# Turning attention outputs by DMA and a layer norm by TensorE in a fused transformer block, with a new order

## The chip, the cores and the metric

One core of one Trainium2 chip. The time is device microseconds (us) of one launch; that of the kernel before is the median of three runs. A profile is one execution taken by the hardware profiler.

The engines: TensorE (PE; its weight loads are listed apart as PEld), VectorE (DVE), ScalarE (ACT), GpSimd (POOL), and SyncE (SP), which here only issues DMAs. Each engine runs its own instructions in the order of the program and waits on semaphores.

## The reference

A transformer block with pre-norm, forward and backward, in bf16, for 2048 tokens of width 512 (32 heads of 16, feed-forward width 1792):

```python
def _A_ref(x, wqkv, wo):            # dilated sliding window: 8 keys, 2 apart
    q, k, v = qkv[0], qkv[1], qkv[2]                       # x @ wqkv
    idx = pos[:, None] - off[None, :]                      # off = arange(8) * 2
    logits = jnp.einsum("bhsd,bhswd->bhsw", q, kg) * scale
    attn = _softmax(jnp.where(mask[None, None, :, :], logits, -1e9), axis=-1)
    o = jnp.einsum("bhsw,bhswd->bhsd", attn, vg)
    return o.transpose(0, 2, 1, 3).reshape(B, S, D) @ wo

def _B_ref(x, w1, b1, w2, b2):
    h = _gelu(jnp.einsum("bsd,df->bsf", x, w1) + b1)
    return jnp.einsum("bsf,fd->bsd", h, w2) + b2

h = x + _A_ref(_layernorm(x), A_wqkv, A_wo)
h2 = h + _B_ref(_layernorm(h), B_w1, B_b1, B_w2, B_b2)
# outputs: h2 and the gradients of x, wqkv, wo, w1, b1, w2, b2 for a given grad_out
```

## The kernel before

The tokens are cut into four chunks of 512 (`c` from 0 to 3, four tiles of 128 rows each). Per chunk the forward pass runs `p1_ln` (first layer norm), `p1_qkv`, `p1_attn`, `p1_o` (attention output), `p1_h` (output projection with `wo`, residual `h`, second layer norm `ln2`), `p2_h` (first feed-forward matmul with `w1`, GELU), `p2_out` (second one, `w2`). The chunks are worked in the order 0, 2, 1, 3. The backward pass is `p2_dg`, `p2_bwd` (matmuls with `w2T` and `w1T`), `p3_go`, `p3_dots`, `p3_bands`, `p3_gl1` (gradient of x, tile `gx`), and `wg_ffn` makes the weight gradients.

Attention is made of bands: VectorE multiplies (`prod`, tile `prbo` in the forward pass), PE sums with a 0/1 matrix (`bsum`, L527), ScalarE copies the sum out (`sink`, L532, tile `ost`). A matmul needs its left operand with the width along the partitions, so `ost` has to be turned into `oT`, and `ln2` into `ln2T`. There are two ways:

- by PE: 16 transposes of 128x128 for each chunk into PSUM, and copies by ScalarE. `turn` (L543) does it for `ost` in two halves of 1024 columns, `to_fm_tiles` (L416) for a layer norm in four tiles of 512.
- by DMA: one transposing transfer of 512 KB on SyncE's queue, `turned` for `ost` and `to_fm_dma` for a layer norm (both through `xload`, L291).

Constants at the end of the file choose the way for each chunk: `FMO` lists the chunks whose `ost` is turned by DMA, `FM2` those whose `ln2` is.

Every step is recorded as an operation first. `emit` then writes the operations out in the order of the table `ORDER`, made ahead of time outside the kernel, with the addresses of `HOMES`. That sets the order on every engine and queue. `emit` also decides the form of most matmuls:

```python
            if o.eng == "PE":
                if o.cls == 4:
                    run.append(i)
                else:
                    if prev == 1 and o.cls == 1:
                        quad.update(run)
                    run, prev = [], o.cls
```

Class 1 operations (band sums, attention sums, the q and k projections) are always issued as four matmuls of 32 columns side by side. A run of ordinary matmuls (class 4) that stands between two class 1 operations is issued in the same form, as four strips (L268); all others are issued full, with 128 columns (L270). A transpose on PE is class 0 and ends a run.

DMA transfers of SyncE's and ScalarE's queues finish on a shared, rotating set of eight semaphores, so an issue may also wait until an earlier transfer has landed, on whichever queue that was.

Of the kernel before, what the change touches and what calls it, by code (L numbers as in the profile page):

```python
# [13 lines left out]
ACT = mybir.ActivationFunctionType  # L14
# [145 lines left out]
def kernel(  # L160
# [30 lines left out]
    NC = S // CH  # L191
# [767 lines left out]
    def p3_gl1(c):  # L959
# [6 lines left out]
        for j in range(TPC):  # L966
# [9 lines left out]
            if j == 0:  # L976
                gx = sb("gx", [P, TPC, D])
            ln_bwd(t, NT + t, j % 2, pair, ps, rstdp, RP, ln1, lambda j=j: ln1()[:, j, :], [(gh_[c], j - 1), (gh_[c], j)], lambda j=j: gh_[c]()[:, j - 1:j + 1, :],
                   gx, lambda j=j: gx()[:, j - 1:j + 1, :], (j - 1, j), "1")
        for j, ap in enumerate(perm_rows(gxf[c * CH:(c + 1) * CH, :])):  # L980
            store(None, lambda ap=ap: ap, gx, lambda j=j: gx()[32 * j:32 * j + 32], 128, tag="gxst")
# [196 lines left out]
FM2 = (1, 2, 3)  # L1178
# [4 lines left out]
FMO = ()  # L1183
# [146 lines left out]
```

## Time and profile before

| what | value |
|---|---|
| median of three runs | 557.82 us (556.07 to 574.06) |
| profiled execution | 557.15 us |
| its span, first to last instruction | 555.4 us |
| mean granted TensorE clock | 0.999 |
| busy PE / DVE / ACT / POOL | 539.7 / 494.2 / 324.2 / 32.4 us |
| PE matmuls | 5568 |
| DMA moved | 126.40 MB, mean 228 GB/s |

The profiled execution is 1.75 us longer than its span: that lies around the first and the last instruction. A busy PE need not be at its peak, since matmuls are pipelined and their ends are modelled. A name such as `ps<-wo,oT` reads: the tile written, then the tiles read.

### The profile page before, as it was taken

To read this page: it belongs to the slowest core of one execution; us is meant where nothing else is said; L and a number is where in the kernel's file an instruction comes from. 1 tells how busy PE (TensorE), PEld (TensorE's weight loads), DVE (VectorE), ACT (ScalarE), POOL (GpSimd) and SP (SyncE) were. 2 spreads that over 40 slices of the span, in tenths; PEclk is the share of its full clock that TensorE was granted. 3 is DMA by queue.
4 is the path that set the end of the run, shared out by engine and by line. 5 is a ranking of instruction groups with operands and counts; after the bars stand their busy time and mean duration, and the time that the engine had idled before them with its cause. 6 is when DMAs were issued, how large, how long until landed. Compare 5 with 4: busy or idle time off the path is not lost. (4 is left out here: it accounts for less than half of the span.)

```text
span 555.4 us, 13067 instructions
## 1 busy us (share of the span) xinstructions
PE 539.7 (97%) x5568; PEld 268.9 (48%) x5568; DVE 494.2 (89%) x648; ACT 324.2 (58%) x503; POOL 32.4 (6%) x38
## 2 busy tenths in 40 slices
PE   7999999999999999999999999999999998999995
PEld 4655554444444444444444444455455554555442
DVE  7999999999999999889885877789879998999992
ACT  4998699887999794996131324042324556633531
POOL 1610100021001000000000000000010001000000
PEclk9999999999999999999999999999999999999999
DMA  8898998975499617298999989999999999778237
GB/s 265 218 289 251 395 368 236 199 228 185 97 268 281 179 34 167 77 152 221 199 210 184 194 183 187 295 212 271 240 357 374 305 335 372 318 272 162 52 72 199
DMA packets 195306, 126.40 MB, mean 228 GB/s; under 512 B 149744, under 2 KB 190896, under 8 KB 193200
## 3 DMA queue, kind: packets, MB, share of 16 engines
q1 hardware_dynamic: 189760, 82.06, 64.5%
q0 software_dynamic: 3312, 41.42, 19.2%
q10 hardware_dynamic: 2176, 2.10, 1.2%
q8 instruction: 43, 0.70, 0.5%
q14 instruction: 15, 0.12, 0.1%
HBM read 55.74 MB, written 35.21 MB: 164 GB/s over the span
## 5 line engine op out<-in xcount | busy, mean ns | idle before, releaser
L270 PE MATMUL ps<-goT,w2T 128*128 128x512 bf16 x224 | 53.6, 379 | 0.8 <-DVE h2s L828 0.5
L270 PE MATMUL ps<-w1T,xb 128*128 128x512 bf16 x224 | 52.9, 379 | 0.0
L270 PE MATMUL ps<-w,gl 128*128 128x512 bf16 x216 | 50.5, 379 | 0.0
L297 ACT CAST wgs<-ps 128x512 bf16<-128x512 f32 (+1 forms) x30 | 16.2, 558 | 57.4 <-PE ps L268 35.7
L270 PE MATMUL ps<-ln2T,w 128*128 128x512 bf16 x188 | 44.2, 379 | 0.7 <-DVE xb L856 0.3
L774 ACT ACTIVATE xb<-ps,b1c 128x512 bf16<-128x512 f32 x56 | 35.7, 692 | 12.8 <-PE ps L270 12.5
L856 DVE SCALAR_TENSOR_TENSOR xb<-xb,ps 128x512 bf16<-128x512 bf16 x56 | 36.6, 685 | 6.2 <-PE ps L270 5.6
L518 DVE TENSOR_TENSOR prbq<-Rq,cfq 128x4096 bf16<-128x4096 bf16 x16 | 36.0, 2288 | 5.0 <-PE ps L487 1.7
L479 DVE TENSOR_TENSOR prb<-got,vw 128x4096 bf16<-128x4096 bf16 x16 | 36.3, 2282 | 2.7 <-PE ps L487 1.4
L518 DVE TENSOR_TENSOR prbv<-Rv,cfv 128x4096 bf16<-128x4096 bf16 x16 | 36.1, 2283 | 2.7 <-PE ps L268 1.8
L518 DVE TENSOR_TENSOR prbk<-Rk,cfk 128x4096 bf16<-128x4096 bf16 x16 | 36.1, 2283 | 0.7 <-PE ps L527 0.7
L518 DVE TENSOR_TENSOR prbo<-Ro,cfo 128x4096 bf16<-128x4096 bf16 x16 | 35.9, 2288 | 0.4 <-DMA k_d<-tmk 0.2
L479 DVE TENSOR_TENSOR prf<-qt,kt 128x4096 bf16<-128x4096 bf16 x16 | 35.5, 2275 | 0.0
L270 PEld LDWEIGHTS <-w2T 128*128 128x128 bf16 x224 | 21.8, 98 | 27.4 <-issue 2.0
L270 PEld LDWEIGHTS <-xb 128*128 128x128 bf16 x224 | 21.9, 98 | 26.4
L270 PEld LDWEIGHTS <-gl 128*128 128x128 bf16 x216 | 20.8, 98 | 25.6 <-issue 1.6
L796 ACT ACTIVATE xb<-xb 128x2048 bf16<-128x2048 bf16 (+1 forms) x16 | 26.8, 1690 | 7.8 <-DVE xb L795 7.7
L626 PE MATMUL ps<-ln1T,wqk 128*32 128x512 bf16 x512 | 30.2, 383 | 0.0
L270 PEld LDWEIGHTS <-w 128*128 128x128 bf16 x188 | 18.1, 97 | 23.0 <-issue 2.5
L268 PE MATMUL ps<-wqkvT,gqkvT 128*32 128x512 bf16 x448 | 27.4, 379 | 1.7 <-ACT gqkvT L297 1.6
L777 ACT ACTIVATE gl<-xb 128x2048 bf16<-128x2048 bf16 (+1 forms) x16 | 26.8, 1697 | 0.0
L792 ACT ACTIVATE x<-xb 128x2048 bf16<-128x2048 bf16 (+1 forms) x16 | 26.6, 1690 | 0.0
(198 smaller groups left out, 1054.0 us busy)
## 6 DMA issues: line engine op xcount, KB each, us to landing
Ro<-v_d POOLq DMA_DIRECT2D x4, 2304.0 KB, 11.2
Rq<-k_d POOLq DMA_DIRECT2D x4, 2304.0 KB, 11.6
Rv<-go_d POOLq DMA_DIRECT2D x4, 2304.0 KB, 14.2
Rk<-q_d POOLq DMA_DIRECT2D x4, 2304.0 KB, 13.4
g_d<-gl SPq DMA_DIRECT2D x9, 512.0 KB, 3.5
gh_d<-xb SPq DMA_DIRECT2D x9, 512.0 KB, 3.4
w<-in_B_w_dram SPq DMA_DIRECT2D x2, 1792.0 KB, 15.0
out_dram<-wgs SPq DMA_DIRECT2D x13, 256.0 KB, 7.1
```

The costliest lines, as they stand in the source:

```text
L268: T.matmul(out[32 * a:32 * a + 32, :], lhsT=l[:, 32 * a:32 * a + 32], rhs=r, start=start, stop=stop, skip_group_check=True)
L270: T.matmul(out, lhsT=l, rhs=r, start=start, stop=stop, skip_group_check=True)
L297: fn = lambda: A.copy(out=ap(), in_=pap())
L479: op("DVE", tt_us(4096), lambda g=g, pr=pr: V.tensor_tensor(out=pr(), in0=ql()[:, g, :].unsqueeze(1).to_broadcast([P, W, 512]), in1=_sub(k ...
L518: V.tensor_tensor(out=pr().rearrange("p a j (d h) -> p a j d h", h=H), in0=_sub(R()[:, o0, 0:1], [[st, 2], [512, 4], [32, DH], [1, H]]), i ...
L626: T.matmul(ps()[32 * a:32 * a + 32, gg * 512:(gg + 1) * 512], lhsT=_sub(wq_()[:, dc, 0:1], [[DH, H]], sel * D + 4 * g + a), rhs=rhs, start ...
L774: op("ACT", act_us(512, 1), lambda f=f, ps=ps, xb=xb, f0=f0: A.activation(out=xb()[:, f - f0, :], in_=ps(), func=ACT.Identity, bias=b1c[:, ...
L777: op("ACT", act_us(N), lambda xb=xb, gl=gl: A.activation(out=fl(gl), in_=fl(xb), func=ACT.Gelu_apprx_tanh), r=[xb], w=[gl], tag="gelu", mo ...
L792: op("ACT", act_us(N), lambda xb=xb, x2=x2: A.activation(out=fl(x2), in_=fl(xb), func=ACT.Square), r=[xb], w=[x2], tag="x2")
L796: op("ACT", act_us(N), lambda xb=xb: A.activation(out=fl(xb), in_=fl(xb), func=ACT.Tanh, scale=GC), w=[xb], tag="tanh", mode=6)
L856: op("DVE", 0.61, lambda f=f, ps=ps, z=z, f0=f0: V.scalar_tensor_tensor(out=z()[:, f - f0, :], in0=z()[:, f - f0, :], scalar=1.0, in1=ps() ...
```

## The change

The attention outputs of chunks 1 and 3 are turned by DMA, no longer by PE. The second layer norm of chunks 1 and 2 is turned by PE tile by tile, no longer by DMA; chunk 3 stays with DMA and chunk 0 with PE. For chunk 3, two of the four stores of `gx` are issued by ScalarE, no longer by SyncE. `ORDER` and `HOMES` are new as a whole (one line is shown).

```diff
-            store(None, lambda ap=ap: ap, gx, lambda j=j: gx()[32 * j:32 * j + 32], 128, tag="gxst")
+            store(None, lambda ap=ap: ap, gx, lambda j=j: gx()[32 * j:32 * j + 32], 128, q="ACT" if c == NC - 1 and j % 2 else "SP", tag="gxst")
...
-FM2 = (1, 2, 3)
+FM2 = (3,)
...
-FMO = ()
+FMO = (1, 3)
...
 ORDER = (
-    8, 22, 0, 11, 12, 23, 1, 7, 10, 6, 9, 48, 364, 27, 13, 49, 50, 26, 51, 44, 61, 28, 2, 62, 40, 25, 3, 45, 29, 41, 24, 46, 52, 42, 43, 53, 363, 15,
...
```

PE, from the last band sum of chunk 1's attention output (`prbo_432`) to that of chunk 3 (`prbo_581`) and on, before. Repeated rows and the weight loads are left out; `oT1` and `oT3` are the turned outputs of chunks 1 and 3, `gl` the GELU's output, `goT` the turned gradient.

```order
L527 MATMUL ps<-prbo_432_34_1774,S4 32x512
...
L270 MATMUL ps<-wo_91_14_372,oT1_441_32_1803 128x512
...
L543 MATMUL ps<-ident,ost_428_33_1765 128x128
...
L270 MATMUL ps<-ln2T2_478_34_1913,w1_226_24_984 128x512
...
L527 MATMUL ps<-prbo_581_41_2197,S4 32x512
...
L270 MATMUL ps<-ln2T1_533_38_2030,w1_226_24_984 128x512
...
L543 MATMUL ps<-ident,ost_576_42_2169 128x128
...
L270 MATMUL ps<-wo_91_14_372,oT3_628_42_2332 128x512
...
L270 MATMUL ps<-w2_295_21_1264,gl_647_38_2370 128x512
...
L270 MATMUL ps<-w1T_596_41_2268,xb_333_28_1394 128x512
```

The same place in the changed kernel, with `prbo_422` and `prbo_580` as those band sums:

```order
L527 MATMUL ps<-prbo_422_38_1772,S4 32x512
...
L270 MATMUL ps<-wo_60_11_274,oT1_439_33_1841 128x512
...
L416 MATMUL ps<-ident,ln2_2_468_31_1906 128x128
...
L270 MATMUL ps<-ln2T2_479_33_1931,w1_217_22_939 128x512
...
L416 MATMUL ps<-ident,ln2_1_517_35_2013 128x128
...
L527 MATMUL ps<-prbo_580_42_2201,S4 32x512
...
L268 MATMUL ps<-ln2T1_537_38_2056,w1_217_22_939 32x512
...
L268 MATMUL ps<-goT_404_37_1659,w2T_346_34_1440 32x512
...
L268 MATMUL ps<-wo_60_11_274,oT3_600_40_2300 32x512
...
L268 MATMUL ps<-w2_278_24_1161,gl_642_39_2510 32x512
...
L268 MATMUL ps<-w1T_589_40_2249,xb_342_33_1419 32x512
```

The transposes of `ost` (L543) are gone for both chunks, those of `ln2` (L416) are new. Between `prbo_422` and the first `wo` matmul on `oT1` stand 30 full matmuls and 8 transposes of other work, between `prbo_580` and the first on `oT3` 160 strips. Since no transpose ends the run behind `prbo_580`, the whole feed-forward up to the next attention sums is issued in strips: over the program L268 has 5376 matmuls in place of 2448, L270 688 in place of 1420, and PE 15530 rows in place of 11138.

SyncE at the same place, before; `ln2T2` and `ln2T1` are the turned layer norms:

```order
L291 DMA_TRANSPOSE goT_430_33_1768<-gor_256_28_1110 128x16x128
L291 DMA_TRANSPOSE w2T_357_30_1496<-in_B_w2_dram 128x4x448
L287 DMA k_d_58<-tmk_203_29_866 128x2x512
L287 DMA g_d0_73<-gl_419_31_1721 128x2x512
L282 DMA xp3_386_32_1568<-in_A_x_dram 32x4x512
L291 DMA_TRANSPOSE ln2T2_478_34_1913<-ln2_2_465_34_1879 128x16x128
```

And in the changed kernel:

```order
L291 DMA_TRANSPOSE w2T_346_34_1440<-in_B_w2_dram 128x4x448
L287 DMA v_d_57<-tmv_239_27_1031 128x2x512
L282 DMA xp1_93_14_373<-in_A_x_dram 32x4x512
L291 DMA_TRANSPOSE oT1_439_33_1841<-ost_421_38_1770 128x16x128
L287 DMA q_d_59<-tmq_340_33_1409 128x2x512
L287 DMA q_d_59<-tmq_427_35_1793 128x2x512
```

Chunk 1's attention output takes the place that chunk 2's layer norm had, closer behind a transpose of `w2T`; chunk 3's stands between two transposes of `w1T`.

VectorE near the start of the program, before; `xt_0` is chunk 0 of x, `xt_13` chunk 1, `ln_0` the normalised chunk 0:

```order
L360 BN_STATS st<-xt_0_1_95 128x6
L361 BN_AGGR mv<-st 128x2
L369 RECIPROCAL rstd<-ve 128x1
L385 TENSOR_SCALAR ln_0_18_7_133<-xt_0_1_95,mv,rstd 128x512 x2
L369 RECIPROCAL rstd<-ve 128x1
L385 TENSOR_SCALAR ln_0_18_7_133<-xt_0_1_95,mv,rstd 128x512
L360 BN_STATS st<-xt_13_5_126 128x6
```

And in the changed kernel, where chunk 1 is `xt_14`:

```order
L360 BN_STATS st<-xt_0_1_95 128x6
L361 BN_AGGR mv<-st 128x2
L360 BN_STATS st<-xt_14_4_123 128x6
L361 BN_AGGR mv<-st 128x2
L369 RECIPROCAL rstd<-ve 128x1
L385 TENSOR_SCALAR ln_0_23_7_136<-xt_0_1_95,mv,rstd 128x512
```

One statistics pair of chunk 1 now stands ahead of the last normalisations of chunk 0.

204 rows, old and new, of tables (HOMES, ORDER) are left out of this document.

## The prediction

> **What bounds the kernel now.** I read the page's engine shares first, then stretches of the span, then who TensorE waits for, then the chain that ended last.
>
> ```profile
> PE 539.7 (97%) x5568; PEld 268.9 (48%) x5568; DVE 494.2 (89%) x648; ACT 324.2 (58%) x503; POOL 32.4 (6%) x38
> ```
>
> TensorE (PE) is busy for 539.7 of 555.4 us and idle for 15.7. VectorE has 494.2 us of work beside it. So an edit can gain only what is idle or slow inside PE's time. The stretches say where that is (us of the stretch, then busy us and instructions of PE, weight loads, VectorE, ScalarE, GpSimd, then clock, DMA share, GB/s):
>
> ```profile
> 0.00:14.00 14.00, 11.18 (x106) 6.03 (x110) 10.13 (x33) 6.56 (x15) 2.22 (x9) 1.00 0.85 266
> 84.00:98.00 14.00, 13.73 (x133) 6.99 (x134) 13.65 (x10) 13.94 (x19) 0.60 (x1) 1.00 0.83 233
> 112.00:126.00 14.00, 13.13 (x73) 6.28 (x72) 12.68 (x25) 11.23 (x14) 3.52 (x4) 1.00 0.75 234
> 440.00:460.00 20.00, 18.38 (x292) 9.92 (x285) 18.97 (x12) 10.05 (x16) 2.12 (x4) 1.00 1.01 333
> 540.00:556.00 16.00, 9.47 (x44) 4.12 (x42) 5.47 (x13) 2.92 (x5) 0.00 (x0) 0.96 0.73 190
> ```
>
> The start costs 14.00 - 11.18 = 2.8 us and the end 15.4 - 9.47 = 5.9 us (the span covers 15.4 of that stretch). That leaves 15.7 - 2.8 - 5.9 = 7.0 us of idle in the middle, in small pieces in the first 140 us, where VectorE is just as full (13.65 of 14), and one of 1.6 at 440 to 460. The longest waits of PE confirm it:
>
> ```profile
> PE ps L268 <- ACT gqkvT L297: 1.6, 1, 1.6
> PE ps L416 <- DVE ln L385: 1.5, 1, 1.5
> ```
>
> PE's own rate depends on how its instructions follow each other. These pieces are from the chain that ended last (start, us, what, count):
>
> ```profile
> 381.53 0.55 PE ps L527 x8
> 385.53 0.43 PE ps L527 x8
> 471.79 0.97 PE ps L270 x4
> 473.65 0.86 PE ps L270 x4
> 494.56 5.18 PE ps L268 x96
> 524.32 25.16 PE ps L270 x116
> ```
>
> L270 is a full 128-column matmul, L268 the same product as four 32-column strips, L527 the band sums, always in strips. Band sums after strips take 0.43 us, after full matmuls 0.55; four full matmuls after strips 0.97, otherwise 0.86 (the pieces at 381.53 and 471.79 stand right behind the other form). So each change of form costs about **0.11 us**. In long runs the forms are equal: 5.18 / 24 = 216 ns per four strips, 25.16 / 116 = 217 ns per full one.
>
> **The change part by part.** Sums are made against the profiled execution, 557.15 us (span 555.4 and 1.75 around it), 0.67 below the median of the runs shown, 557.82.
>
> *The swapped transposes.* Four chunk turns change sides.
>
> ```profile
> L543 PE MATMUL ps<-ident,ost 128*128 128x128 bf16 x64 | 4.9, 219 | 0.4 <-ACT ost L532 0.4
> L416 PE MATMUL ps<-ident,ln 128*128 128x128 bf16 x32 | 3.1, 221 | 2.9 <-DVE ln L385 1.5 <-ACT kt L297 1.0 <-ACT ln L381 0.2
> L297 ACT COPY oT<-ps 128x1024 bf16<-128x1024 bf16 x8 | 8.1, 1011 | 0.8 <-PE ps L543 0.7
> L297 ACT COPY ln2T<-ps 128x512 bf16<-128x512 bf16 x4 | 2.2, 582 | 0.0
> ```
>
> Each turn is 16 PE transposes of 128x128. Chunks 1 and 3 lose theirs at L543 (32), chunks 2 and 1 gain theirs at L416 (32): PE's work is unchanged. ScalarE loses 4 copies of 1.011 us and gains 8 of 0.582: +0.6 us, hidden, since it is idle for 2.8 of 14 us at 112 to 126; 0.6 if that cover were gone. SyncE issues two transposes fewer and two more: no change in DMA bytes. **0**, between 0 and +0.6.
>
> *The wait that is added.* The output projection of chunks 1 and 3 (L268/L270, `wo`) must now wait for all of a DMA transpose. Before, chunk 1's looked like this on PE:
>
> ```profile
> 110.16 0.60 PE L527 MATMUL ps<-prbo,S 128*32 128x512 bf16 x8
> 113.75 1.03 PE L270 MATMUL ps<-wo,oT 128*128 128x512 bf16 x4
> ```
>
> The order rows put, between the last band sum and the first `wo` matmul, 30 full matmuls and 8 transposes for chunk 1 (30 x 0.217 + 0.45 = 6.9 us) and 160 strips for chunk 3 (40 x 0.216 = 8.6 us). Needed in that time: the sink's copy and the transfer.
>
> ```profile
> L532 ACT ACTIVATE ost<-ps 128x512 bf16<-128x512 f32 x16 | 9.3, 599 | 1.4 <-PE ps L527 1.4
> ln2T<-ln SPq DMA_TRANSPOSE x3, 4.3
> DMA to landing us min/median/max: 4.3/5.1/6.0
> DMA to landing us min/median/max: 4.4/9.0/13.6
> ```
>
> The nearest row is the removed transfer itself, `ln2T`, same size and shape, same place in the program: 4.3 us. The third line is `goT`, issued around it and later, the fourth `ghT`, in the crowded stretch after 290 us. With 0.6 for the band sum, 0.6 for the sink: 5.5 us at 4.3, 7.2 at 6.0, 14.8 at 13.6. I take 4.3: **0**; at 6.0 it is 0.3 for chunk 1, at 13.6 it is 7.9 + 6.2 = 14.1 us. Behind the waiting matmul everything on PE stands still, and VectorE's residual sums of the chunk with it; behind the transpose on SyncE stand stores of q and k, which nobody needs for 100 us. GpSimd's queue keeps its steps there.
>
> A rule to weigh here: the Trainium skill, "DMA: Bandwidth & Descriptors", section "Latency and other measured facts", gives transposing transfers an effective 261 GB/s; by it the 512 KB would land in about 2 us (an estimate from that figure). The trace differs: 4.3 us at best, and the measurement decides.
>
> *The strips.* PE's program grows by 4392 rows. 732 matmuls of the feed-forward turn from full into strips (the order rows show why: no transpose of chunk 3 ends the run any more). In long runs that is -1 ns each by the two rows above, 732 x -1 = -0.7 us; the group rows bound the other side:
>
> ```profile
> L268 PEld LDWEIGHTS <-gqkvT 128*32 128x32 bf16 x448 | 12.2, 97 | 14.1 <-ACT gqkvT L297 2.1 <-DMA gqkvT<-gks 0.6
> L270 PEld LDWEIGHTS <-xb 128*128 128x128 bf16 x224 | 21.9, 98 | 26.4
> 405.00:425.00 20.00, 20.00 (x380) 10.93 (x368) 17.43 (x14) 5.81 (x13) 1.48 (x3) 1.00 0.99 386
> q8 instruction: 43, 0.70, 0.5%
> ```
>
> Four strip loads cost 4 x 12.2/448 = 109 ns, a full load 98: 11 ns more, hidden below 216 ns of matmul; exposed it would be 732 x 11 = 8.1 us. The stretch 405 to 425 holds 380 matmuls, nearly all strips, with DMA 0.99 busy and no idle PE, so neither loads nor the fetching of instructions (0.70 MB in all now) showed there. **0**, between -0.7 and +8.1.
>
> *Fewer changes of form.* Counted over PE's order, full and strip runs alternate 46 times before and 34 times after: 12 x 0.11 = 1.3 us. Net, eleven of the twelve lie in the first 140 us, where PE also waits for VectorE, so I count half: **-0.7**, between -1.3 and 0.
>
> *The start.* VectorE now takes chunk 1's first statistics ahead of the last two normalisations of chunk 0:
>
> ```profile
> 8.42 0.41 DVE L385 TENSOR_SCALAR ln<-xt,mv,rstd 128x512 bf16<-128x512 bf16 x1
> 8.75 0.68 DVE L360 BATCH_NORM_STATS2 st<-xt 128x6 f32<-128x512 bf16 x1
> 9.47 0.18 DVE L361 BATCH_NORM_AGGREGATE mv<-st 128x2 f32<-128x6 f32 x1
> ```
>
> That is up to 0.8 us later for PE's first projection; later VectorE is the one that is waited for, and its work is only reordered. **+0.4**, between 0 and 0.8.
>
> *The rest of the order.* The 1.6 us wait at 459 has this chain:
>
> ```profile
> 439.54 18.76 DMA ln1b<-ln_d
> 458.37 0.43 ACTq L287
> 458.85 1.02 ACT gqkvT L297
> 459.91 2.77 PE ps L268 x48
> ```
>
> A store on ScalarE's queue was held until a load had landed, and the copies that PE needed stood behind it. The new order places that store and those loads anew; whether the meeting recurs can't be read off, so half of PE's 1.6 us: **-0.8**, between -1.6 and 0.
>
> *The end.* Two of the last four `gx` stores go to ScalarE's queue.
>
> ```profile
> 549.06 2.46 SPq L287 DMA_DIRECT2D out_dram<-gx  x3
> 550.12 0.38 ACTq L287 DMA_DIRECT2D out_dram<-wgsq  x1
> 553.00:554.00 1.00, 0.00 (x0) 0.00 (x0) 0.00 (x0) 0.00 (x0) 0.00 (x0) 1.00 0.32 110
> ```
>
> SyncE issues its last store at 551.0 and DMA runs until about 553.3. ScalarE's last store, at 550.12, needs PE's last result in both kernels, so the 0.9 us between the two issues is the most that can go. ScalarE has room: 2.92 us busy of the last 16. **-0.5**, between -0.9 and 0; should a `gx` store hold ScalarE up for VectorE's last sum, PE's last groups still take longer.
>
> Sum: -0.7 + 0.4 - 0.8 - 0.5 = -1.6 us, so 557.15 - 1.6 = **555.5 us**.
>
> **The rivals.** *Slower:* the DMA turns land late. If SyncE's queue, which holds the `w2T` and `w1T` transposes just ahead, delays them as `ghT` was delayed, PE stands for 14.1 us: 571.3 us, the gains being lost in the same stretch. Against it: 4.3 us in that place. It decides above 5.7 us to landing for chunk 1 and 7.4 for chunk 3. *Strips with open weight loads:* 555.5 + 8.1 = 563.6 us. The Trainium skill, "TensorEngine Tiling (Array Packing)", section "Gotcha 2: Feature Incompatibilities", says that column tiling excludes Fast Weight Load, which speaks against strips. The trace agrees as to the load (109 against 98 ns) but not as to the time (216 against 217). *A worse order:* as many new waits as the old middle had, 7.0 us: 562.5. The first 140 us, with both engines full, leave room for that. *Faster:* all of the middle's idle, 7.0 us, and all 46 changes of form, 46 x 0.11 = 5.1 us, go: 545.1. Nothing is left to take beyond that, and the new order keeps 34 changes. *Nothing at all:* every gain was covered, 557.2, inside the forecast's own range.
>
> **How the numbers follow.** Chances: forecast 0.70 (own range 551.5 to 559.5), worse order 0.11, late turns 0.07, open loads 0.06, faster 0.06. The range reaches down by all four gains (-1.3 - 1.6 - 0.9 - 0.7 = -4.5) and half of the middle's idle (-3.5) to 549.1, and up over the worse order and the open loads to 564; outside lie the late turns and the faster case, with an edge. Two per cent, about what a measurement of this kernel can tell from no change, is 11.1 us: below 546.0 only the faster case (0.05), above 568.3 only the late turns (0.07), within 0.88.
>
> **What would show it.** PE busy still near 540 us; L543 on `ost` with 32 and L416 on `ln` with 64 instructions; strips from about 140 to 330 us at 93 to 95 matmuls' worth per 20 us; `oT` transposes of some 4 to 5 us and no wait of PE on them; no 18 us load ahead of a store on ScalarE; last DMA within 4 us of PE's last matmul. I am wrong if PE shows waits on `oT` of over 3 us, if four strips take over 225 ns in the feed-forward, or if waits on VectorE in the first 140 us change by more than 4 us.

## The result, and the profile after

The changed kernel takes 552.98 us (median of 4 runs, 552.61 to 553.85), the kernel before beside it 557.71. The ratio is 0.9935, with a 95% interval of 0.9908 to 0.9963: some 3.6 us faster, far below the two per cent that count as a change here. (The ratio leaves out slow runs such as one of 574.06 us of the kernel before; the medians are 4.7 us apart.) The profiled executions are 557.15 and 553.85 us, 3.3 apart; forecast was 1.6, with 555.5 us and a range of 549.1 to 564.0.

The page of the changed kernel, engine shares first:

```profile
PE 537.2 (97%) x7764; PEld 286.2 (52%) x7764; DVE 494.0 (90%) x648; ACT 324.1 (59%) x507; POOL 24.7 (4%) x38
q8 instruction: 60, 0.98, 0.8%
```

TensorE still sets the time, idle for 14.6 of 551.8 us (15.7 before). The strips are there (7764 matmuls), and with them more instructions to fetch (0.98 MB against 0.70). Stretches of the changed kernel, in the columns of the prediction's:

```profile
0.00:14.00 14.00, 10.29 (x98) 6.46 (x102) 11.10 (x36) 6.90 (x16) 1.88 (x8) 1.00 0.88 282
84.00:98.00 14.00, 14.00 (x168) 7.03 (x160) 13.91 (x8) 13.76 (x19) 0.60 (x1) 1.00 0.93 211
112.00:126.00 14.00, 13.81 (x77) 6.71 (x76) 13.43 (x26) 12.08 (x17) 3.38 (x4) 1.00 1.00 354
140.00:160.00 20.00, 18.78 (x344) 9.60 (x336) 19.80 (x30) 18.33 (x23) 0.59 (x1) 1.00 0.83 147
440.00:460.00 20.00, 20.00 (x314) 10.73 (x307) 19.84 (x11) 14.37 (x26) 1.60 (x3) 1.00 1.00 314
```

The start has lost 0.9 us (10.29 busy, 11.18 before). The holes at 84 to 98 and 112 to 126 are smaller (idle 0 and 0.19 us, before 0.27 and 0.87), the one of 1.6 at 440 to 460 is gone, and a new one of 1.2 us stands at 140 to 160. PE's longest waits:

```profile
PE ps L311 <- DVE wz L307: 2.0, 1, 2.0
PE ps L270 <- DVE mx L690: 1.2, 1, 1.2
PE ps L416 <- DVE ln L385: 0.9, 1, 0.9
PE ps L268 <- DMA oT<-ost: 0.9, 1, 0.9
```

The wait on `oT` (0.9 us, at 154.97 us) and one of 0.3 us on `gl` at 158.93 make the new hole. The first and the third of these lines belong to the start; the wait on `mx` lies at 32.6 us.

Of the signs that the prediction named, the counts came: 32 transposes of `ost` and 64 of `ln` on PE, and strips in the whole feed-forward (the next section has a row). Two did not hold: PE does wait on `oT`, and the last DMA ends 4.6 us behind PE's last matmul (550.5 - 545.9), not within 4.

```profile
L543 PE MATMUL ps<-ident,ost x32: 219/219/219, 55.5 to 88.5; 128*128 128x128 bf16 x32
L416 PE MATMUL ps<-ident,ln x64: 216/219/230, 5.7 to 133.6; 128*128 128x128 bf16 x64
```

To see which differences last I took a **delay** from both traces: the start of each PE operation minus the sum of the durations that the source of the kernel books for all PE operations ahead of it (0.2157 us for a full product or four strips, 0.445 for a band sum of eight strips, 0.056 for a transpose; the sum is 528.2 us in both kernels). It grows by whatever PE waits or loses. By place in that sum:

| planned us on PE | what stands there | before | after | after minus before |
|---|---|---|---|---|
| 11.7 | first projections of chunk 0 | 5.49 | 6.01 | +0.52 |
| 57 | attention of chunk 2 | 7.92 | 7.89 | -0.03 |
| 95 | end of chunk 1's band sums | 12.60 | 10.55 | -2.05 |
| 105 | output projection, chunk 1 | 13.73 | 11.03 | -2.70 |
| 141 | just ahead of it for chunk 3 | 14.85 | 11.76 | -3.09 |
| 160 | feed-forward | 15.27 | 13.67 | -1.60 |
| 320 | end of the feed-forward | 17.25 | 15.86 | -1.39 |
| 430 | backward attention | 18.68 | 16.97 | -1.71 |
| 450 | the wait of 1.6 us before | 20.53 | 17.28 | -3.25 |
| 520 | last weight gradients | 21.09 | 17.55 | -3.54 |

So nothing is gained in the first 57 us, 2.7 us come from 57 to 105 and 0.4 more by 141, 1.5 are given back around chunk 3's turn, and 1.5 come back at 450 us. The experiments ask which of these belong to every execution, and to which part of the change.

### The profile page after: what moved, and what is told of

Same layout as the page of the kernel before. It is cut to its first block, busy times and chain, and to the rows that moved or that the text cites. A ratio compares the mean times of both kernels' runs of the same rounds, so it can differ in the third digit from the quotient of the medians.

```text
span 551.8 us, 17461 instructions
## 1 busy us (share of the span) xinstructions
PE 537.2 (97%) x7764; PEld 286.2 (52%) x7764; DVE 494.0 (90%) x648; ACT 324.1 (59%) x507; POOL 24.7 (4%) x38
## 5 line engine op out<-in xcount | busy, mean ns | idle before, releaser
L268 PE MATMUL ps<-w1T,xb 128*32 128x512 bf16 x896 | 53.1, 379 | 0.6 <-DVE h2s L828 0.4
L268 PE MATMUL ps<-goT,w2T 128*32 128x512 bf16 x832 | 50.5, 379 | 0.3 <-ACT xb L774 0.3
L268 PE MATMUL ps<-w,gl 128*32 128x512 bf16 x776 | 46.3, 379 | 0.5 <-ACT gl L777 0.3
L268 PEld LDWEIGHTS <-xb 128*32 128x32 bf16 x896 | 26.2, 97 | 23.1 <-issue 1.2
L268 PEld LDWEIGHTS <-w2T 128*32 128x32 bf16 x832 | 24.1, 97 | 21.3 <-issue 0.6
L268 PEld LDWEIGHTS <-gl 128*32 128x32 bf16 x776 | 21.3, 97 | 21.8 <-ACT gl L777 2.3
L268 PE MATMUL ps<-wqkvT,gqkvT 128*32 128x512 bf16 x512 | 31.0, 379 | 0.0
L270 PE MATMUL ps<-ln2T,w 128*128 128x512 bf16 x120 | 27.4, 379 | 0.0
L268 PE MATMUL ps<-ln2T,w 128*32 128x512 bf16 x416 | 24.6, 379 | 0.0
```

Source lines behind the costliest of these rows:

```text
L268: T.matmul(out[32 * a:32 * a + 32, :], lhsT=l[:, 32 * a:32 * a + 32], rhs=r, start=start, stop=stop, skip_group_check=True)
L270: T.matmul(out, lhsT=l, rhs=r, start=start, stop=stop, skip_group_check=True)
```

## The experiments

**The strips.** The long run of ordinary matmuls is issued full.

```diff
-                    if prev == 1 and o.cls == 1:
+                    if prev == 1 and o.cls == 1 and len(run) < 100:
```

> The changed kernel, except that the one long run of ordinary matmuls (184 operations, the feed-forward behind chunk 3's band sums) is issued full instead of in strips; two more changes of form, everything else in the same order. Theory (strips cost nothing when weight loads lie under 216 ns of matmul): no difference, 553.0 us give or take 0.6 (two changes of form, +0.2; 732 matmuls at 1 ns, +0.7). Rival (the strips' weight loads, 11 ns longer per product, are partly exposed in the feed-forward): faster by up to 8.1 us, 545 us.

Measured: 552.74 us, ratio to the kernel before 0.9925 (0.9894 to 0.9957): the same time as with strips. The same stretch of the feed-forward, in the changed kernel and then in this one:

```profile
200.00:280.00 80.00, 79.34 (x1464) 42.63 (x1460) 73.95 (x150) 49.70 (x71) 0.00 (x0) 1.00 0.88 177
```

```profile
200.00:280.00 80.00, 79.79 (x370) 36.08 (x369) 74.77 (x154) 50.74 (x75) 0.00 (x0) 1.00 0.85 183
```

1464 strips are 366 products, against 370 full ones in 80 us. Four times as many weight loads (42.63 us against 36.08) lie below the matmuls. The rival with open loads (8.1 us) is out, and the medians show nothing. The profiles show a little: from 160 to 304 us of planned time the delay grows by 1.4 to 1.8 us in three with strips there (the changed kernel and two variants below; a fourth, the run with chunk 3's turn moved, loses more for other reasons), and by 0.8 to 0.9 in five without. The Trainium skill, "TensorEngine Tiling (Array Packing)", section "Gotcha 2: Feature Incompatibilities", says that column tiling excludes Fast Weight Load; the longer loads fit that, and here they cost less than 1 us.

**The last stores.** All four are issued by SyncE again.

```diff
-  store(..., q="ACT" if c == NC - 1 and j % 2 else "SP", tag="gxst")
+  store(..., tag="gxst")
```

> The changed kernel, except that all four last stores of gx are issued by SyncE again. Theory of the prediction (SyncE's issue row sets the end): slower by 0.5 us, between 0 and 0.9, so 553.5 us. Rival (the new profile has the same 5.9 us behind PE's last matmul as before, with two issues for gx ahead of wgsq on ScalarE): no change or up to 0.7 us faster, 552.3 to 553.0 us.

Measured: 552.69 us, 0.9941 (0.9918 to 0.9964): no change, as its rival said. In the chain that ended last, the changed kernel's ScalarE now issues `gx` stores between its last copies:

```profile
541.42 0.70 DVE gx L570
...
542.15 0.68 ACTq L287
...
542.87 0.60 ACT wgsq L297
...
543.49 0.38 ACTq L287
...
543.91 0.58 ACTq L287
```

The first of them waits for VectorE's sum, which ends at 542.12, and ScalarE's next copy of PE's results stands behind it. From PE's last matmul to the end of the span it was 5.9 us before (555.4 - 549.47) and is 5.9 after (551.8 - 545.93); with all stores on SyncE it is 5.4 (550.8 - 545.38).

**The price of a change of form.** No ordinary matmul is issued in strips.

```diff
-                    if prev == 1 and o.cls == 1:
+                    if False and prev == 1 and o.cls == 1:
```

> The changed kernel with no ordinary matmul issued as strips, so that band sums and the like are the only strips: 130 changes of form in place of 34. Theory (0.11 us for each change, in full): 553.0 + 96 x 0.11 = 563.5 us. Half of it, if part lies beside waits that are there anyway: 558.3 us. Rival (the difference seen at the changes was something else, a wait for a bank for instance): 553.0 us, or less because 1376 strips fewer are loaded.

Measured: 560.96 us, ratio to the kernel before 1.0072 (1.0049 to 1.0095), so 8.0 us slower than the changed kernel: 0.083 us for each of 96 changes. (PE issues 7764 - 3732 = 4032 matmuls fewer, not the 1376 of the expectation.) Where the changes stand decides:

| planned us on PE | changes, changed kernel | changes here | growth of the delay here, less that in the changed kernel | for each |
|---|---|---|---|---|
| 0 to 160 | 19 | 36 | 12.04 - 11.69 = 0.35 | 0.02 |
| 160 to 320 | 0 | 7 | 1.49 - 2.19 = -0.70 | none: the strips are gone |
| 320 to 528 | 15 | 87 | 9.13 - 1.69 = 7.44 | 0.10 |

PE's rows in the last stretch, here and then in the changed kernel:

```profile
480.80 0.61 PE L527 MATMUL ps<-prbq,S 128*32 128x512 bf16 x8
481.35 1.04 PE L270 MATMUL ps<-gqs,ln1b 128*128 128x512 bf16 x4
482.23 1.03 PE L270 MATMUL ps<-wqkvT,gqkvT 128*128 128x512 bf16 x4
483.18 0.61 PE L527 MATMUL ps<-prbq,S 128*32 128x512 bf16 x8
```

```profile
484.51 0.60 PE L527 MATMUL ps<-prbq,S 128*32 128x512 bf16 x8
484.95 0.60 PE L527 MATMUL ps<-prbv,S 128*32 128x512 bf16 x8
```

A band sum ahead of a full group lasts 481.35 - 480.80 = 0.55 us until the next start, ahead of another strip 0.44; a full group ahead of a band sum 0.95, otherwise 0.88. The price of 0.11 us is real in the last stretch, where PE hardly waits for another engine. In the first 160 us, where PE waits for VectorE and ScalarE anyway, it is nearly nothing.

**The swaps alone, in the old order.** The kernel before with the new choice of turns. I placed the new steps by hand: the transfers right behind the last copy of the band sums, PE's transposes of `ln2` and chunk 1's output projection a few matmul groups behind them.

```diff
-FM2 = (1, 2, 3)
+FM2 = (3,)
-FMO = ()
+FMO = (1, 3)
```

> The kernel before with the swapped transposes alone: chunks 1 and 3 of the attention output by DMA, chunks 1 and 2 of the second layer norm by PE, in the old order, where only the output projection of chunk 1 moves some 8 operations back so that it can wait for the turn; gx stores all on SyncE. 42 changes of form (27 in the first 140 us), the long feed-forward run in strips. Theory (the swaps are worth 0, the new order around them brought the gain): 557.3 us, between 556.3 and 559.5, with the wait of 1.6 us near 460 us still there and PE's delay at 140 us still near 14.5 us. Rival (the swaps themselves free the first 140 us, as TensorE no longer waits for the sink and ScalarE in two halves): 554.5 us, with the delay at 140 us near 11.8.

Measured: 572.0 us, 1.0269 (1.0228 to 1.031): 15 us slower, which neither theory had. A second attempt placed the same steps with more care:

> The kernel before with the swapped transposes alone, as in the run of that kind before, but placed with care: the PE transposes of ln2 stand where their inputs are ready (eight matmul groups behind chunk 1's last band sum), three groups of other work are drawn ahead of them, chunk 1's output projection stands behind them, and chunk 3's transposing transfer stands ahead of a w1T transpose. Theory (the swaps themselves are worth about 0, the 14 us of the first attempt were the price of bad places): 557.5 us, between 556 and 560. Rival (the old order has no room for the swaps: more than a few waits stay around 115 to 160 us): over 562 us.

Measured: 576.3 us, 1.0335 (1.0292 to 1.0378). The delays of both attempts:

| planned us on PE | before | swaps, first | swaps, second |
|---|---|---|---|
| 95 | 12.60 | 13.39 | 12.93 |
| 105 | 13.73 | 19.17 | 13.67 |
| 141 | 14.85 | 24.58 | 22.74 |
| 160 | 15.27 | 30.63 | 32.34 |
| 520 | 21.09 | 33.80 | 35.77 |

The loss falls between 95 and 160 us. SyncE's issues, then VectorE and PE there, in the second attempt:

```profile
120.23 0.34 SPq L1117 DMA_DIRECT2D rst<-r_d  x1
136.81 0.67 SPq L287 DMA_DIRECT2D out_dram<-h2s  x1
137.53 0.58 SPq L1117 DMA_DIRECT2D rst<-r_d  x1
153.69 0.40 SPq L287 DMA_DIRECT2D gh_d<-xb  x1
159.09 2.36 SPq L291 DMA_TRANSPOSE oT<-ost  x1
161.50 8.17 SPq L291 DMA_TRANSPOSE w1T<-in_B_w_dram  x2
```

```profile
120.77 0.69 DVE L747 TENSOR_TENSOR h<-ps,xp 128x512 bf16<-128x512 f32 x1 [2.61 <-ACT ln2T L297]
...
136.10 0.69 DVE L828 TENSOR_TENSOR h2s<-ps,h 128x512 bf16<-128x512 f32 x1
...
174.40 0.69 DVE L747 TENSOR_TENSOR h<-ps,xp 128x512 bf16<-128x512 f32 x1 [3.39 <-DMA xp<-in_A_x_dram]
```

```profile
136.24 3.56 PE L270 MATMUL ps<-ln2T,w 128*128 128x512 bf16 x8 [2.33 <-DVE xb L856]
...
168.91 1.05 PE L268 MATMUL ps<-wo,oT 128*32 128x512 bf16 x16 [2.12 <-DMA oT<-ost]
...
178.78 1.90 PE L268 MATMUL ps<-w1T,xb 128*32 128x512 bf16 x16 [4.50 <-issue]
```

VectorE's residual sums of chunk 1 (L747) now come late and hold up what stands behind them: VectorE stands 2.61 us at 120.77 and gets to `h2s` only at 136.10. SyncE's queue, in order, waits 16 us for that (its store goes at 136.81), and again 16 us for VectorE's `xb` (153.69). The turn of chunk 3 and the loads of `w1T` and `xp` come in one crowd behind that, and PE and VectorE wait for each of them (the wait of 4.50 us has no releaser in the row; a transpose of `w1T` landed at 178.69 and PE started at 178.78). A waiting queue alone doesn't explain the loss: in the changed kernel SyncE issues nothing from 118.7 to 143.97 us, and PE stays busy. The granted clock falls too, to 0.92 from 137 to 154 us and 0.83 from 172 to 180; how much of the loss is its share wasn't separated. So the old order holds no room for these swaps, at least not in these two placements; a better one by hand wasn't tried.

**The turns of `ost`, undone in the new order.** First chunk 3 alone is turned by PE again (its transposes end the long run of strips, which the first experiment priced at under 1 us), then chunks 1 and 3. I placed the transposes by hand behind the band sums; everything else keeps the new order. The edit of the first run, then of the second (`ORDER` and `HOMES` left out):

```diff
-FMO = (1, 3)
+FMO = (1,)
```

```diff
-FMO = (1, 3)
+FMO = ()
```

> The changed kernel, except that chunk 3's attention output is turned by PE again: 16 transposes in two halves behind the band sums, two copies of 1.0 us on ScalarE, and the long feed-forward run full instead of strips as a consequence. Theory (the DMA turn of chunk 3 costs its wait of 0.9 to 1.3 us and gives nothing): 1.0 us faster than the changed kernel, 551.7 us. Rival (ScalarE is full between 140 and 165 us, so its two copies, 2.0 us, come on top ahead of the GELU that TensorE already waits 0.3 us for): slower than the changed kernel by 0.8 to 1.5 us, 553.5 to 554.3 us, with waits of TensorE on gl.

Measured: 553.13 us, 0.995 (0.9932 to 0.9968): neither, the same time as the changed kernel. PE's delay is 13.65 at 160 us, against 13.67, with 16 more transposes (0.9 us) booked ahead of that. In place of the wait for the transfer PE now waits 0.24 us for ScalarE's copy of `oT` at 150.94 and 0.94 us at 159.81, which the profile puts down to VectorE's residual sum. The 0.9 us come back in the feed-forward, which is issued full here.

> The changed kernel, except that no attention output is turned by DMA: chunks 1 and 3 are turned by PE again, the transposes placed in the new order behind the band sums, so that only the second layer norm's swap and the order remain. Theory (the gain of 3 us sits in the new order of the first 104 us, and the turns of ost are worth nothing either way): 553.1 us, between 552.5 and 554, with PE's delay at 104 us near 10.7 as in the changed kernel. Rival (the DMA turn of chunk 1 earns the 1.0 us between 95 and 104 us by relieving ScalarE and TensorE there): 554.1 us and a delay of 11.7 at 104 us; if both turns earned the whole gain, 556 us.

Measured: 555.46 us (all twelve runs between 555.34 and 555.53), 0.9974 (0.9947 to 1.0001): 2.3 us more than with chunk 3 alone, a loss between the two rivals. The delay is 11.07 at 104 us, not 10.7, and 12.52 at 110, against 11.00 with chunk 1 turned by DMA. The stretch 112 to 126 with the DMA turn of chunk 1 (the run before), then without it, and PE's wait in it:

```profile
112.00:126.00 14.00, 13.81 (x77) 6.71 (x75) 13.43 (x26) 12.05 (x17) 3.36 (x4) 1.00 1.02 358
```

```profile
112.00:126.00 14.00, 12.89 (x72) 6.08 (x71) 11.60 (x22) 12.68 (x17) 3.06 (x4) 1.00 0.64 221
```

```profile
116.97 0.40 PE L416 MATMUL ps<-ident,ln 128*128 128x128 bf16 x4 [0.80 <-ACT ln L381]
117.68 0.40 PE L416 MATMUL ps<-ident,ln 128*128 128x128 bf16 x4 [0.31 <-ACT ln L381]
```

ScalarE is busy for 12.68 of 14 us instead of 12.05, its layer norm starts at 116.12 instead of 113.36, and PE waits 0.92 us more here. With 16 more transposes on PE (16 x 0.056 = 0.9 us) and 1.4 us of delay by 520 us (17.54 against 16.14) that is the 2.3. So the DMA turn of chunk 1 earns 2.3 us in the new order, that of chunk 3, with the strips that come with it, nothing.

What is left without either is the new order and the swap of `ln2`, and it isn't told from the kernel before: its interval reaches 1.0001. PE waits less (delay 12.52 against 13.74 at 110 us) but has 32 transposes more than either kernel (32 x 0.056 = 1.8 us), and the two cancel. PE's work ends at 547.71 us there, at 547.77 in the kernel before with one store moved (below), at 545.41 with chunk 1 turned by DMA and at 545.93 in the changed kernel. The gain needs both: the turns in the old order lose 15 us and more, and the new order without them gains nothing that shows. (It was made for the DMA turns; a better place for the transposes wasn't tried.)

**The place of chunk 3's turn on SyncE.** In the changed kernel the transfer is issued between two transposes of `w1T`:

```profile
143.97 1.52 SPq L291 DMA_TRANSPOSE w1T<-in_B_w_dram  x1
146.10 3.35 SPq L291 DMA_TRANSPOSE oT<-ost  x1
149.49 4.93 SPq L291 DMA_TRANSPOSE w1T<-in_B_w_dram  x1
```

```profile
154.97 1.26 PE L268 MATMUL ps<-wo,oT 128*32 128x512 bf16 x20 [0.89 <-DMA oT<-ost]
```

From issue to PE's start it takes 8.9 us; chunk 1's landed 4.3 us after its issue. One operation of `ORDER`, the first `w1T` transpose (511), moves behind the turn (476):

```diff
-    475, 595, 511, 724, 719, 601, 466, 604, 468, 699, 602, 469, 708, 476, 715,
+    475, 595, 724, 719, 601, 466, 604, 468, 699, 602, 469, 708, 476, 511, 715,
```

> The changed kernel, except that one w1T transpose, which stood just ahead of chunk 3's transpose of ost on SyncE, stands just behind it; nothing else is moved. Theory (the 0.9 to 1.3 us that TensorE waits for oT at 155 us is a price of the place on SyncE's queue, and is lost for good because nothing behind it absorbs it): 1.0 us faster than the changed kernel, 551.8 us, with oT's issue near 1.6 us in place of 3.35 and PE's delay at the feed-forward 1.0 us smaller. Rival (the wait is only handed on, to the w1T transposes or to ScalarE's copies in the feed-forward): 552.7 us, the same as the changed kernel.

Measured: 554.66 us, 0.9994 (0.997 to 1.0018): slower by 1.7 us. Its profile is of the longest of twelve runs (559.4 us), so how much of what it shows belongs to a median run stays open. SyncE, VectorE, ScalarE and PE:

```profile
147.32 2.90 SPq L291 DMA_TRANSPOSE oT<-ost  x1
150.40 6.42 SPq L291 DMA_TRANSPOSE w1T<-in_B_w_dram  x2
...
173.74 1.18 SPq L287 DMA_DIRECT2D g_d<-gl  x2
```

```profile
179.72 0.69 DVE L793 TENSOR_SCALAR ga<-x 128x2048 bf16<-128x2048 bf16 x1 [2.30 <-DMA g_d<-gl]
```

```profile
183.91 2.86 ACT L796 ACTIVATE xb<-xb 128x2048 bf16<-128x2048 bf16 x2 [3.95 <-DVE xb L795]
```

```profile
155.74 2.77 PE L268 MATMUL ps<-wo,oT 128*32 128x512 bf16 x48 [0.42 <-DMA oT<-ost]
...
188.62 1.53 PE L268 MATMUL ps<-w,gl 128*32 128x512 bf16 x16 [2.07 <-ACT gl L777]
```

The turn still takes 8.4 us, now with two `w1T` transposes right behind it. The wait for it falls from 0.89 to 0.42 us, and the next one, on `gl`, grows from 0.33 to 0.79: so far it is handed on, as the rival said. But then more is lost. Everything later on SyncE is issued later, a store of `gl` among it; VectorE waits 2.3 us for that store, ScalarE 4.0 for VectorE, and PE 2.1 for ScalarE. Neither theory foresaw that.

**The wait at 459 us.** In the kernel before, the store on ScalarE's queue moves 28 places later, behind the copies that it held up (1886 is that store).

```diff
-    1316, 1510, 1886, 1418,
+    1316, 1510, 1418,
...
-    1888, 1349, 1889, 1438,
+    1888, 1349, 1886, 1889, 1438,
```

> The kernel before, except that one store of the output-projection weight gradient on ScalarE's queue stands 28 operations later, behind the copies that TensorE waits for near 459 us. Theory (the store was held until the 18.8 us load on SyncE had landed, by the shared completion semaphores, and the copies stood behind it): the wait of 1.6 us at 459 us goes and nothing behind takes it back, 1.5 to 1.8 us faster than the kernel before. Rival (the wait is given back, since VectorE's work behind it sets the time, or the next load holds the store again): no difference, and the wait shows up further down.

Measured: 556.47 us, 1.0011 (0.999 to 1.0033). In the profile the wait is gone (delay 18.37 at 450 us, 20.53 before), and the span is 553.8 us in place of 555.4; in the medians there is nothing. So I had the unchanged kernel profiled again:

> The kernel before, unchanged, profiled once more. The run with the store moved later lost the 1.6 us wait at 459 us in its profile and yet took the same median time. Theory (the wait is part of every execution, and the moved store paid elsewhere): the wait of 1.6 us on ScalarE's gqkvT copies is there again, behind a load of over 15 us, and the span is near 555.4 us. Rival (how long that load takes differs from execution to execution, and the profiled one was unlucky): no such wait or a much shorter one, and a span of 553.5 to 554.5 us.

Measured: 555.99 us, 0.9993 (0.9975 to 1.0011). In this execution PE stood still for 7.0 us from 501.6 us on, so only what lies ahead of that is read: the delay at 450 us is 18.26, without the wait. The store that was held until 458.37 in the first profile:

```profile
453.38 0.42 ACTq L287 DMA_DIRECT2D out_dram<-wgso  x1
```

The wait is a matter of one execution, as the rival said. The load that held the store landed 18.8 us after its issue in the first profile and 11.0 in this one. In the two attempts at the swaps, which keep the old order there, it took 9.4 and 12.6 us, and PE's delay doesn't grow from 430 to 450 us.

**The start.** VectorE's order at the start is put back: operation 0 fills the warm-up tile, 169 takes chunk 1's first statistics.

```diff
-    8, 10, 22, 7, 21, 12, 11, 0, 15,
+    8, 10, 22, 7, 0, 21, 12, 11, 15,
...
-    5, 169, 54, 59, 55, 41, 60, 63, 64, 42, 43, 57,
+    5, 54, 59, 55, 41, 60, 63, 64, 42, 43, 169, 57,
```

> The changed kernel, except that VectorE writes the tile of the warm-up matmuls first and takes chunk 1's first statistics behind the last normalisation of chunk 0, as in the kernel before. Theory (the 0.5 us that the changed kernel starts later is absorbed by 57 us, where both kernels have the same delay): no difference, 552.7 us, PE's first projection some 0.5 us earlier and the delay at 62 us again 8.3. Rival (the term of the prediction, +0.4, lasts to the end): 552.2 to 552.3 us.

Measured: 553.58 us, 0.9955 (0.9934 to 0.9976): no gain. But the edit did not bring the start forward in its profile (delay 6.22 at 11.7 us, 6.01 in the changed kernel), so the run decides nothing. That a late start is swallowed rests on the delays of 0.52 at 11.7 and -0.03 at 57 us in the table above; a later one is so only in part: the run with chunk 3's turn moved started 2.0 us later than the changed kernel (8.05) and still had 1.3 of it at 57 us (9.15 against 7.89).

**Two parts undone together.**

> The changed kernel with two of its parts undone together: the long feed-forward run issued full (two more changes of form) and all gx stores on SyncE. Theory (both are worth nothing, as each was alone: 552.7 us): 552.7 us, between 552.2 and 553.2. Rival (the profiles of the two single runs show the feed-forward 0.8 us and the end 0.5 us shorter, which a median of a dozen runs hid): 551.6 us.

Measured: 552.61 us, 0.9937 (0.9907 to 0.9967): the theory's number, and no version that beats the changed kernel.

## Why the prediction was right, and where it was wrong

The sign was right and the time lies inside the range; the gain was twice the forecast, and it came from other terms than those that were added up. That the number came near is luck.

- **Swapped transposes, 0.** PE's work is the same, as said. But the 0 was wrong: chunk 1's turn is worth 2.3 us in the new order, 0.9 of PE's transposes (which those of `ln2` take back) and 1.4 of waits. "Hidden, since ScalarE is idle for 2.8 of 14 us" failed for ScalarE's copies: where chunk 1's two come back, the layer norm behind them starts 2.8 us later and PE waits for it. An engine that is idle for a fifth of a stretch is not idle where the copies must stand.
- **The wait for the turns, 0.** Right for chunk 1 (4.3 us, no wait). For chunk 3 PE waited 0.89 us: 8.9 us after the issue instead of 4.3, with transposes of `w1T` next to it. That is above the 7.4 us from which the wait was to begin, and inside the bounds given (0 to 14.1). The rival of late turns is real: in the old order, where chunk 3's turn landed 9.1 and 9.7 us after its issue, the attempts cost 15 and 19 us, though not by that wait alone.
- **Strips, 0.** Right within 1 us: 552.74 us without them, and 0.5 to 1 us in the profiles.
- **Fewer changes of form, -0.7.** The price was right, its place wrong. 11 of the 12 changes that went lie in the first 140 us, where one is worth 0.02 us: 0.2 in all. Between 160 and 320 us there are two fewer, behind 320 one more: 0.1 us.
- **The start, +0.4.** It was 0.5 us later at 11.7 us and nothing at 57.
- **The rest of the order, -0.8.** This step failed. I looked only at the one long wait, which belonged to one execution, and took nothing for the many short ones. Those gave the gain: 2.7 us between 57 and 105 us and 0.4 by 141. The order does not give it alone: without the DMA turns 1.2 us of it are left at 110 us, and the added transposes eat them. Order and turns were priced as separate terms, and it is their meeting that counts.
- **The end, -0.5.** Wrong, 0: the first store on ScalarE waits for VectorE and stands ahead of ScalarE's last copies, the very mishap that I named and put down as covered.

In sum, from the profiled executions: -3.1 up to 141 us, +1.5 around chunk 3's turn, and -1.5 at 450 us by chance of the execution before; the rest within 0.5. Without that chance about 2 us are left, by two profiles: the kernel before with its store moved and the changed one end PE's work at 547.77 and 545.93 us. That is no more than the DMA turn of chunk 1 earns. The lowest of many runs agree, 554.1 us before and 552.2 with the change (the run with all stores on SyncE). The medians are 3.3 to 3.6 apart, so a typical run of the kernel before seems to lose over 1 us more; where, apart from the held store, stays open.

## What to carry to other kernels

A DMA in place of an engine's work is as late as the queue that it stands in: price it with what that queue waits for just ahead of it, and with the transfers beside it, not with its own transfer time. Try the parts of a change alone and together: here the turns lost in one order and gained in another, and neither the order nor the turns gained without the other. A price per event, like that of a change of form, counts only where its engine sets the time. And before a single long wait in a profile is counted as a term, look for it in a second execution.

## What the hardware showed that I had not expected

- A 512 KB transposing transfer landed in 4.3 us where the transposes nearest to it were issued 6 us before and 36 us after. With transposes of `w1T` issued next to it, and the DMA engines full (share 1.24 from 146 to 155 us), it took 8.4 to 8.9 us (about 59 GB/s at 8.9, from its issue to PE's start). Which of the neighbours slows it wasn't separated. The Trainium skill, "DMA: Bandwidth & Descriptors", section "Latency and other measured facts", with its 261 GB/s, is further off here than in the prediction's row.
- DMA engines that stand nearly still need not cost anything. While SyncE's queue waited, their share was 0.05 for 14 us in the first attempt of the swaps, where PE is busy for 11.87 us, and 0.07 in the changed kernel, where it is busy for 13.89:

```profile
126.00:140.00 14.00, 11.87 (x55) 5.18 (x53) 11.71 (x23) 7.51 (x11) 1.93 (x1) 1.00 0.05 21
```

```profile
126.00:140.00 14.00, 13.89 (x103) 6.62 (x104) 13.76 (x18) 12.97 (x23) 0.00 (x0) 1.00 0.07 26
```

- A store on ScalarE's queue, behind a load on SyncE's, was issued at 458.37 in one execution and at 453.38 in another of the same program, which was 0.6 us ahead just before it (delay 18.11 against 18.67 at 430 us). The load landed 18.8 and 11.0 us after its issue.
